# Linear attention followed by a squared-ReLU FFN: tokens tiled as 9p+j, K=64 matmuls in row groups, the max of k folded into v, the max of q subtracted in PSUM, the FFN interleaved with the next batch

## The chip, the cores and the metric

The kernel runs on one core of a Trainium2 chip (trn2). The metric is the device time of one execution in microseconds; lower is better. Executions of one kernel agree closely: the runs of the kernel before span 476.36 to 479.01 us in the rounds used here, about half a percent.

TensorE (PE in the profile) multiplies, DVE is VectorE, ACT is ScalarE, POOL is GpSimd. In these traces a matmul that waits holds up those issued after it: in the changed kernel PE stands idle for 1.32 us before the kv matmul at 83.11 us, which waits for scaled v, while FFN matmuls that need nothing from it come only afterwards, the first at 85.19 us. The order itself is chosen by the scheduler of the programming layer, which moves independent instructions into gaps that it expects.

## The reference, cut to what matters

```python
# q, k, v: (8 batches, 8 heads, 576 tokens, 64); w_phi: (64, 128)
def phi(x):
    proj = einsum('bhsd,df->bhsf', x, w_phi)
    proj = proj - max(abs(proj), axis=-1)          # over the 128 features
    return concatenate([exp(proj), exp(-proj)])
q_p, k_p = phi(q), phi(k)
kv  = einsum('bhsf,bhsd->bhfd', k_p, v);  z = sum(k_p, axis=2)
num = einsum('bhsf,bhfd->bhsd', q_p, kv); den = einsum('bhsf,bhf->bhs', q_p, z) + 1e-6
x   = (num / den) as (4608 tokens, 512)
out = relu(x @ w_in)**2 @ w_out                    # 512 -> 2048 -> 512
```

Subtracting m before both exponentials scales both halves of a token's features by exp(-m): exp(p-m) is exp(p) times exp(-m), but exp(-(p-m)) is exp(-p) times exp(+m). So the max of q is not a common factor of the two halves in the literal formula. The kernel before does not subtract it from q at all, and passes the comparison with the reference. The inputs (normal, times 0.1) make the maxima small. That is a property of this reference's data and tolerance, and it should be kept in mind.

## The kernel before

One batch has 576 tokens, cut in five chunks: four of 128 rows and one of 64. Per batch (cut):

```python
# transposes of q and k, two heads at a time; the fifth one has only 64 rows
for j, dstT in ((0, qT), (1, kT)):
    for pr in range(NPAIR):
        for isc, (s0, ssz) in enumerate(SCH):
            nc.tensor.transpose(out=tp[:, s0:s0+ssz], in_=xin[:ssz, isc, j, 2*pr:2*pr+2, :]..., ...)
        nc.scalar.activation(out=dstT[:, pr, :], in_=tp, func=ACT.Copy)
for isc, (s0, ssz) in enumerate(SCH):
    # 8 matmuls with K=64 -> pj; max; subtract; two Exp
    nc.vector.tensor_reduce(out=m[:ssz], in_=pj[:ssz], op=ALU.max, apply_absolute_value=True)
    nc.vector.tensor_tensor(out=ksh[:ssz], in0=pj[:ssz], in1=m..., op=ALU.subtract)
    nc.scalar.activation(out=kphp[:ssz, isc], in_=ksh[:ssz], func=ACT.Exp, scale=1.0)
    nc.scalar.activation(out=kphn[:ssz, isc], in_=ksh[:ssz], func=ACT.Exp, scale=-1.0)
    # 8 matmuls with K=64 -> pjq; two Exp of it; no max for q
    ...
    drain_op()            # one of the four FFN-out tiles (16 matmuls) of the chunk before
for hi in range(2):
    for pg in range(2):
        kv = ps.tile([P, 2, 2, D + 1], F32, tag="kv", bufs=2, ...)
        for pl in range(2):
            for pn, kph in ((0, kphp), (1, kphn)):
                for isc, (s0, ssz) in enumerate(SCH):      # K = 128,128,128,128,64
                    nc.tensor.matmul(out=kv[:, pl, pn, :],
                        lhsT=kph[:ssz, isc, hi, pr, :], rhs=va[:ssz, isc, h, :],
                        start=(isc == 0), stop=(isc == NSC - 1))
        nc.scalar.activation(out=kv_sb[...], in_=kv[...], func=ACT.Copy)
for isc, (s0, ssz) in enumerate(SCH):
    # 16 matmuls -> nd; reciprocal; multiply; 4 transposes -> xT
    ...
    if isc == ISC_RDY[b]:
        moe_hp(b)         # 64 FFN-in matmuls of 512 columns
```

Of the kernel before, what the change touches and what calls it, by code (L numbers as in the profile page):

```python
# [12 lines left out]
ACT = mybir.ActivationFunctionType  # L13


@with_exitstack
def kernel(
# [13 lines left out]
    Dh, Fd = w_phi.shape  # L31
    DM, DF = moe_w_in.shape
    NTOK = B * S
    P = 128
    NPAIR = H // 2
    KC1 = DM // P
    KC2 = DF // P
    SCH = [(i * P, min(P, S - i * P)) for i in range((S + P - 1) // P)]
    NSC = len(SCH)
    TCHUNK = 512  # L40
    NMC = NTOK // TCHUNK

    consts = ctx.enter_context(tc.tile_pool(name="consts", bufs=1))
    big = ctx.enter_context(tc.tile_pool(name="big", bufs=1))
# [4 lines left out]
    wphi2 = consts.tile([P, Fd], BF16)  # L49
    nc.gpsimd.dma_start(out=wphi2[0:Dh, :], in_=w_phi)  # L50
    nc.gpsimd.dma_start(out=wphi2[Dh : 2 * Dh, :], in_=w_phi)

    win = consts.tile([P, KC1, DF], BF16)
    wout = consts.tile([P, KC2, DM], BF16)

    def load_moe_weights():
        nc.gpsimd.dma_start(out=win, in_=moe_w_in.rearrange("(kc p) m -> p kc m", p=P))
        nc.gpsimd.dma_start(out=wout, in_=moe_w_out.rearrange("(kc p) n -> p kc n", p=P))

    xT = big.tile([P, KC1, NTOK], BF16)  # L60

    dmab = ctx.enter_context(tc.tile_pool(name="dmab", bufs=2))
    perb = ctx.enter_context(tc.tile_pool(name="perb", bufs=1))
    work = ctx.enter_context(tc.tile_pool(name="work", bufs=2))
    moeb = ctx.enter_context(tc.tile_pool(name="moeb", bufs=2))
    ps = ctx.enter_context(tc.tile_pool(name="ps", bufs=1, space=bass.MemoryType.PSUM))

    def load_inputs(b):
        xin = dmab.tile([P, NSC, 2, H, D], BF16, tag="xin")
        va = dmab.tile([P, NSC, H, D + 1], BF16, tag="va")  # L70
        nc.gpsimd.memset(va[:, :, :, D : D + 1], 1.0)  # L71
        for j, src in enumerate((q, k)):
            for isc, (s0, ssz) in enumerate(SCH):
                nc.gpsimd.dma_start(  # L74
                    out=xin[:ssz, isc, j],
                    in_=src[b, :, s0 : s0 + ssz, :].rearrange("h s d -> s h d"),
                )
        for isc, (s0, ssz) in enumerate(SCH):
            nc.gpsimd.dma_start(  # L79
                out=va[:ssz, isc, :, :D],  # L80
                in_=v[b, :, s0 : s0 + ssz, :].rearrange("h s d -> s h d"),
            )
        return xin, va

    pend = []

    def moe_hp(mc_i):
        t0 = mc_i * TCHUNK
        h2 = moeb.tile([P, KC2, TCHUNK], BF16, tag="h2", bufs=1)
        for mc in range(KC2):  # L90
            hp = ps.tile([P, TCHUNK], F32, tag="kv", bufs=2)
            for kc in range(KC1):
                nc.tensor.matmul(  # L93
                    out=hp,
                    lhsT=win[:, kc, mc * P : (mc + 1) * P],
                    rhs=xT[:, kc, t0 : t0 + TCHUNK],
                    start=(kc == 0), stop=(kc == KC1 - 1),
                )
            hr = moeb.tile([P, TCHUNK], BF16, tag="hr")
            nc.scalar.activation(out=hr, in_=hp, func=ACT.Relu)  # L100
            nc.vector.tensor_tensor(out=h2[:, mc], in0=hr, in1=hr, op=ALU.mult)
        for tt in range(TCHUNK // P):
            pend.append((mc_i, tt, h2))

    def moe_op(mc_i, tt, h2):
        t0 = mc_i * TCHUNK + tt * P
        op = ps.tile([P, DM], F32, tag="kv", bufs=2)
        for mc in range(KC2):
            nc.tensor.matmul(  # L109
                out=op, lhsT=h2[:, mc, tt * P : tt * P + P], rhs=wout[:, mc, :],  # L110
                start=(mc == 0), stop=(mc == KC2 - 1),
            )
        ot = moeb.tile([P, DM], F32, tag="ot", bufs=3)
        nc.vector.tensor_copy(out=ot, in_=op)  # L114
        nc.sync.dma_start(out=out[t0 : t0 + P, :], in_=ot)

    def drain_op():
        if pend:
            moe_op(*pend.pop(0))

    ISC_RDY = [(((bb + 1) * TCHUNK - 1) - bb * S) // P for bb in range(B)]

    nxt = load_inputs(0)
    load_moe_weights()

    for b in range(B):
        xin, va = nxt
        if b + 1 < B:
            nxt = load_inputs(b + 1)

        qT = perb.tile([P, NPAIR, S], BF16, tag="qT")
        kT = perb.tile([P, NPAIR, S], BF16, tag="kT")
        for j, dstT in ((0, qT), (1, kT)):
            for pr in range(NPAIR):
                tp = ps.tile([P, S], BF16, tag="t2", bufs=2,
                             padded_shape=[None, 1024])
                for isc, (s0, ssz) in enumerate(SCH):
                    nc.tensor.transpose(  # L138
                        out=tp[:, s0 : s0 + ssz],
                        in_=xin[:ssz, isc, j, 2 * pr : 2 * pr + 2, :].rearrange(  # L140
                            "s h d -> s (h d)"),
                        identity=ident[:ssz, :ssz],
                    )
                nc.scalar.activation(out=dstT[:, pr, :], in_=tp, func=ACT.Copy)  # L144

        kphp = perb.tile([P, NSC, 2, NPAIR, Fd], BF16, tag="kphp")
        kphn = perb.tile([P, NSC, 2, NPAIR, Fd], BF16, tag="kphn")
        qphp = perb.tile([Fd, 2, NPAIR, S], BF16, tag="qphp")
        qphn = perb.tile([Fd, 2, NPAIR, S], BF16, tag="qphn")
        for isc, (s0, ssz) in enumerate(SCH):  # L150
            pj = ps.tile([P, 2, NPAIR, Fd], F32, tag="pj", bufs=2)
            for hi in range(2):
                for pr in range(NPAIR):
                    nc.tensor.matmul(  # L154
                        out=pj[:ssz, hi, pr, :],
                        lhsT=kT[hi * Dh : (hi + 1) * Dh, pr, s0 : s0 + ssz],
                        rhs=wphi2[hi * Dh : (hi + 1) * Dh, :],
                        start=True, stop=True,
                    )
            m = work.tile([P, 2, NPAIR], F32, tag="m")  # L160
            nc.vector.tensor_reduce(out=m[:ssz], in_=pj[:ssz], axis=AX.X,  # L161
                                    op=ALU.max, apply_absolute_value=True)
            ksh = work.tile([P, 2, NPAIR, Fd], BF16, tag="ksh")
            nc.vector.tensor_tensor(out=ksh[:ssz], in0=pj[:ssz],  # L164
                                    in1=m[:ssz].to_broadcast([ssz, 2, NPAIR, Fd]),
                                    op=ALU.subtract)
            nc.scalar.activation(out=kphp[:ssz, isc], in_=ksh[:ssz],  # L167
                                 func=ACT.Exp, scale=1.0)
            nc.scalar.activation(out=kphn[:ssz, isc], in_=ksh[:ssz],  # L169
                                 func=ACT.Exp, scale=-1.0)  # L170
            pjq = ps.tile([Fd, 2, NPAIR, P], F32, tag="pj", bufs=2)
            for hi in range(2):
                for pr in range(NPAIR):
                    nc.tensor.matmul(  # L174
                        out=pjq[:, hi, pr, :ssz],
                        lhsT=wphi2[hi * Dh : (hi + 1) * Dh, :],
                        rhs=qT[hi * Dh : (hi + 1) * Dh, pr, s0 : s0 + ssz],
                        start=True, stop=True,
                    )
            nc.scalar.activation(out=qphp[:, :, :, s0 : s0 + ssz],  # L180
                                 in_=pjq[:, :, :, :ssz], func=ACT.Exp, scale=1.0)
            nc.scalar.activation(out=qphn[:, :, :, s0 : s0 + ssz],  # L182
                                 in_=pjq[:, :, :, :ssz], func=ACT.Exp, scale=-1.0)
            drain_op()

        kv_sb = perb.tile([P, 2, NPAIR, 2, D + 1], BF16, tag="kv_sb")
        for hi in range(2):
            for pg in range(2):
                kv = ps.tile([P, 2, 2, D + 1], F32, tag="kv", bufs=2,
                             padded_shape=[None, None, None, P])  # L190
                for pl in range(2):
                    pr = 2 * pg + pl
                    h = 2 * pr + hi
                    for pn, kph in ((0, kphp), (1, kphn)):
                        for isc, (s0, ssz) in enumerate(SCH):
                            nc.tensor.matmul(  # L196
# [9 lines left out]
        for isc, (s0, ssz) in enumerate(SCH):  # L206
# [31 lines left out]
            if isc == ISC_RDY[b]:  # L238
                moe_hp(b)
# [36 lines left out]
```

## Time and profile before

| | before |
|---|---|
| median of 3 runs (before the prediction) | 477.82 us (476.75 to 478.83) |
| span of the profiled run | 476.3 us |
| period of one batch | about 50.6 us |
| FFN matmuls, 128 per batch, 216 to 218 ns start to start | 28.2 us of each period |
| first FFN matmul | 58.7 us |

The page of the profile, parts 1 and 2: busy microseconds with their share of the span, then rows of 40 slices in which a digit is the busy share in tenths, and PEclk is the clock that TensorE was granted, in tenths.

```profile
PE 425.1 (89%) x3552; PEld 237.4 (50%) x3552; DVE 214.4 (45%) x340; ACT 301.8 (63%) x441; POOL 106.0 (22%) x138
...
PE   2533999999998999899989999899989997999996
...
PEclk9999999959997799869995999689976999699999
```

The same page's chain of work that ended last, by engine and then by line:

```profile
PE 73%; ACT 8%; DVE 8%; DMA 5%; POOL 4%; issue 1%; DVEq 0%; POOLq 0%; ACTq 0%
PE hp L93 23%; PE op L109 23%; PE kv L196 12%; DMA xin<-in_q_dram 5%; PE tp L138 4%; PE nd L211 3%; PE nd L216 3%; ACT kphp L167 3%; DVE ksh L164 2%; DVE m L161 2%; PE xtp L231 2%; POOL xin L74 2%; ACT qT L144 2%; ACT hr L100 1%; PE pj L154 1%
```

TensorE bounds the kernel. hp and op (the FFN) are 46% of the chain, and the first attention line is kv with 12%. Now the stretches of one period, by windows of time: length, then busy time and count on each engine, granted clock, share of DMA and GB/s. The first row is a period. The others follow one batch: transposes with the first half of kv, the second half of kv, and most of nd.

```profile
core 0: us, PE busy (x) PEld busy (x) DVE busy (x) ACT busy (x) POOL busy (x), PEclk, DMA share, GB/s
177.50:228.10 50.60, 48.88 (x431) 27.89 (x428) 25.62 (x41) 36.46 (x54) 12.83 (x16) 0.87 0.64 57
245.10:254.30 9.20, 7.48 (x85) 5.25 (x85) 3.03 (x3) 7.84 (x14) 0.00 (x0) 0.71 0.09 31
254.30:258.30 4.00, 4.00 (x42) 2.74 (x41) 0.00 (x0) 0.82 (x2) 0.00 (x0) 0.50 0.00 0
258.30:263.60 5.30, 5.24 (x82) 4.66 (x82) 2.59 (x7) 2.77 (x5) 4.87 (x7) 0.59 1.00 66
```

PE is "busy" all through the second half of kv, yet at half the clock and with 42 matmuls in 4.00 us. The timeline of PE shows a second reason beside the clock (start, length, engine, line, operation, operands, rows*columns of the weights, moving operand, count). This is a stretch at full clock, with a single K=64 matmul between groups of four with K=128:

```profile
44.51 0.23 PE L196 MATMUL kv<-va,kphp 64*128 64x65 bf16 x1
44.67 0.40 PE L196 MATMUL kv<-va,kphn 128*128 128x65 bf16 x4
45.01 0.23 PE L196 MATMUL kv<-va,kphp 64*128 64x65 bf16 x1
45.17 0.40 PE L196 MATMUL kv<-va,kphn 128*128 128x65 bf16 x4
```

A group of five takes 0.50 us (44.51 to 45.01), and the K=64 one alone holds 0.16 us until the next starts.

### The profile page before, as it was taken

What the parts mean: (1) busy time and instruction counts of PE and PEld (TensorE: products, weight loads), DVE (VectorE), ACT (ScalarE), POOL (GpSimd) and SP (SyncE); (2) the same over time, 40 slices, a digit from 0 to 9 for tenths busy, and PEclk for the clock granted to TensorE, in tenths of its full rate; (3) what the DMA queues carried; (4) which work ended last, traced back from release to release, by engine and by line L of the source; (5) the groups of instructions that cost most, each with busy time, mean ns of one, the idle gap of its engine ahead of it and who ended that gap; (6) DMA issues with size and microseconds to landing.
All of it is one profiled execution on the core that took longest, in us unless ns stands there. A gap on an engine that the chain in (4) does not pass through costs nothing.

```text
span 476.3 us, 8350 instructions
## 1 busy us (share of the span) xinstructions
PE 425.1 (89%) x3552; PEld 237.4 (50%) x3552; DVE 214.4 (45%) x340; ACT 301.8 (63%) x441; POOL 106.0 (22%) x138
## 2 busy tenths in 40 slices
PE   2533999999998999899989999899989997999996
PEld 1312744475445744574447554565456443644442
DVE  0360346716732457534661567156633575252331
ACT  2692578947946478946894678657883787371440
POOL 9804747028000730055002800030000000000000
PEclk9999999959997799869995999689976999699999
DMA  9999999619010991169011901070110011001101
GB/s 83 164 202 163 101 94 94 95 10 137 6 59 30 76 76 45 44 45 107 23 67 13 138 4 66 22 51 1 49 41 1 2 45 44 1 1 45 44 23 67
DMA packets 120485, 28.36 MB, mean 60 GB/s; under 512 B 113280, under 2 KB 115328, under 8 KB 120448
## 3 DMA queue, kind: packets, MB, share of 16 engines
q0 software_dynamic: 115264, 18.39, 53.0%
q1 hardware_dynamic: 5184, 9.44, 5.3%
q8 instruction: 28, 0.46, 0.4%
q14 instruction: 9, 0.07, 0.1%
HBM read 36.77 MB, written 9.44 MB: 97 GB/s over the span
## 4 chain that ended last, share of the span: by engine, by line
PE 73%; ACT 8%; DVE 8%; DMA 5%; POOL 4%; issue 1%; DVEq 0%; POOLq 0%; ACTq 0%
PE hp L93 23%; PE op L109 23%; PE kv L196 12%; DMA xin<-in_q_dram 5%; PE tp L138 4%; PE nd L211 3%; PE nd L216 3%; ACT kphp L167 3%; DVE ksh L164 2%; DVE m L161 2%; PE xtp L231 2%; POOL xin L74 2%; ACT qT L144 2%; ACT hr L100 1%; PE pj L154 1%
## 5 line engine op out<-in xcount | busy, mean ns | idle before, releaser
L93 PE MATMUL hp<-xT,win 128*128 128x512 bf16 x576 | 127.4, 379 | 0.7 <-ACT hr L100 0.2
L100 ACT ACTIVATE hr<-hp 128x512 bf16<-128x512 f32 x144 | 85.8, 599 | 55.4 <-PE hp L93 55.2
L93 PEld LDWEIGHTS <-win 128*128 128x128 bf16 x576 | 55.7, 98 | 66.9 <-issue 2.3
L138 PE MATMUL tp<-ident,xin 128*128 128x128 bf16 (+1 forms) x320 | 44.3, 255 | 30.5 <-DMA xin<-in_q_dram 18.9
L161 DVE TENSOR_REDUCE m<-pj 128x8 f32<-128x1024 f32 (+1 forms) x40 | 48.6, 1215 | 24.7 <-PE pj L154 24.7
L222 DVE RECIPROCAL rden<-nd 128x8 f32<-128x8 f32 (+1 forms) x40 | 8.1, 203 | 105.1 <-PE nd L216 104.7
L114 DVE COPY ot<-op 128x512 f32<-128x512 f32 x36 | 24.9, 692 | 59.4 <-PE op L109 59.4
L164 DVE TENSOR_TENSOR ksh<-pj,m 128x1024 bf16<-128x1024 f32 (+1 forms) x40 | 48.9, 1222 | 2.9
L167 ACT ACTIVATE kphp<-ksh 128x1024 bf16<-128x1024 bf16 (+1 forms) x40 | 42.3, 1058 | 11.9 <-DVE ksh L164 11.9
L138 PEld LDWEIGHTS <-xin 128*128 128x128 bf16 (+1 forms) x320 | 26.6, 110 | 43.6 <-DMA xin<-in_q_dram 20.6
L180 ACT ACTIVATE qphp<-pjq 128x1024 bf16<-128x1024 f32 (+1 forms) x40 | 37.2, 931 | 16.2 <-PE pjq L174 16.2
L71 POOL MEMSET va<- 128x40 bf16 x8 | 2.4, 300 | 178.0 <-PE kv L196 178.0
L169 ACT ACTIVATE kphn<-ksh 128x1024 bf16<-128x1024 bf16 (+1 forms) x40 | 41.9, 1048 | 0.0
L196 PE MATMUL kv<-va,kphp 128*128 128x65 bf16 (+1 forms) x320 | 36.1, 232 | 6.3 <-ACT kphp L167 6.2
L74 POOL DMA_DIRECT2D xin<-in_k_dram x40 | 34.2, 926 | 18.8 <-DMA wout<-in_moe_w_out_dram 10.4
L182 ACT ACTIVATE qphn<-pjq 128x1024 bf16<-128x1024 f32 (+1 forms) x40 | 37.6, 939 | 0.0
L74 POOL DMA_DIRECT2D xin<-in_q_dram x40 | 33.9, 908 | 9.1 <-PE tp L138 9.1
L196 PE MATMUL kv<-va,kphn 128*128 128x65 bf16 (+1 forms) x320 | 35.4, 240 | 0.2 <-ACT kphn L169 0.2
L202 ACT ACTIVATE kv_sb<-kv 128x260 bf16<-128x260 f32 x32 | 12.4, 388 | 35.5 <-PE kv L196 34.8
L79 POOL DMA_DIRECT2D va<-in_v_dram x40 | 33.7, 886 | 1.5 <-POOL va L71 1.5
L211 PE MATMUL nd<-kv_sb,qphp 128*128 128x65 bf16 (+1 forms) x320 | 33.3, 221 | 0.0
L216 PE MATMUL nd<-kv_sb,qphn 128*128 128x65 bf16 (+1 forms) x320 | 33.2, 222 | 0.0
(52 smaller groups left out, 528.4 us busy)
## 6 DMA issues: line engine op xcount, KB each, us to landing
out_dram<-ot SPq DMA_DIRECT2D x36, 256.0 KB, 2.0
xin<-in_q_dram POOLq DMA_DIRECT2D x32, 128.0 KB, 4.6
xin<-in_k_dram POOLq DMA_DIRECT2D x32, 128.0 KB, 4.6
va<-in_v_dram POOLq DMA_DIRECT2D x32, 128.0 KB, 5.0
win<-in_moe_w_in_dram POOLq DMA_DIRECT2D x1, 2048.0 KB, 15.0
wout<-in_moe_w_out_dram POOLq DMA_DIRECT2D x1, 2048.0 KB, 25.5
xin<-in_q_dram POOLq DMA_DIRECT2D x8, 64.0 KB, 4.2
xin<-in_k_dram POOLq DMA_DIRECT2D x8, 64.0 KB, 4.2
```

The source lines that it names most:

```text
L74: nc.gpsimd.dma_start(out=xin[:ssz, isc, j], in_=src[b, :, s0 : s0 + ssz, :].rearrange("h s d -> s h d"),)
L93: nc.tensor.matmul(out=hp, lhsT=win[:, kc, mc * P : (mc + 1) * P], rhs=xT[:, kc, t0 : t0 + TCHUNK], start=(kc == 0), stop=(kc == KC1 - 1),)
L100: nc.scalar.activation(out=hr, in_=hp, func=ACT.Relu)
L109: nc.tensor.matmul(out=op, lhsT=h2[:, mc, tt * P : tt * P + P], rhs=wout[:, mc, :], start=(mc == 0), stop=(mc == KC2 - 1),)
L138: nc.tensor.transpose(out=tp[:, s0 : s0 + ssz], in_=xin[:ssz, isc, j, 2 * pr : 2 * pr + 2, :].rearrange("s h d -> s (h d)"), identity=iden ...
L161: nc.vector.tensor_reduce(out=m[:ssz], in_=pj[:ssz], axis=AX.X, op=ALU.max, apply_absolute_value=True)
L164: nc.vector.tensor_tensor(out=ksh[:ssz], in0=pj[:ssz], in1=m[:ssz].to_broadcast([ssz, 2, NPAIR, Fd]), op=ALU.subtract)
L167: nc.scalar.activation(out=kphp[:ssz, isc], in_=ksh[:ssz], func=ACT.Exp, scale=1.0)
L169: nc.scalar.activation(out=kphn[:ssz, isc], in_=ksh[:ssz], func=ACT.Exp, scale=-1.0)
L196: nc.tensor.matmul(out=kv[:, pl, pn, :], lhsT=kph[:ssz, isc, hi, pr, :], rhs=va[:ssz, isc, h, :], start=(isc == 0), stop=(isc == NSC - 1),)
L211: nc.tensor.matmul(out=nd[:ssz, hi, pr, :], lhsT=qphp[:, hi, pr, s0 : s0 + ssz], rhs=kv_sb[:, hi, pr, 0, :], start=True, stop=False,)
L216: nc.tensor.matmul(out=nd[:ssz, hi, pr, :], lhsT=qphn[:, hi, pr, s0 : s0 + ssz], rhs=kv_sb[:, hi, pr, 1, :], start=False, stop=True,)
```

## The change

The intent: tile the 576 tokens as 9p+j (64 partitions, nine tokens each), so that a batch is nine blocks of 64 tokens without a remainder and DMA runs are 2304 bytes in place of 256; put two K=64 matmuls side by side in the two row groups; take reduction and subtraction of k's max out of the way of the exponentials by scaling v with exp(-m) and exp(+m); subtract q's max inside PSUM by a small matmul (the kernel before leaves it out); and issue the FFN of chunk c in small units between the steps of the attention of batch c+1. The core of the diff (cut):

```diff
-    SCH = [(i * P, min(P, S - i * P)) for i in range((S + P - 1) // P)]
+    NJ = S // 64
+    def rows(src, b):
+        return src[b].rearrange("(pr hi) (p j) d -> hi p pr (j d)", hi=2, j=NJ)
...
-            nc.vector.tensor_tensor(out=ksh[:ssz], in0=pj[:ssz], in1=m..., op=ALU.subtract)
-            nc.scalar.activation(out=kphp[:ssz, isc], in_=ksh[:ssz], func=ACT.Exp, scale=1.0)
+            absmax(mk, pj, nj, at)                    # DVE, no longer ahead of the Exp
+            nc.scalar.activation(out=kp[:, :, :w], in_=pj[:, :, :w], func=ACT.Exp, scale=1.0)
+            nc.scalar.activation(out=kn[:, :, :w], in_=pj[:, :, :w], func=ACT.Exp, scale=-1.0)
+            pj = project(qT[gi], nj)                  # only for the max of q
+            absmax(mq, pj, nj, at)
...
+        # va[s] = [v * exp(-/+ m), exp(-/+ m)]: six multiplications per batch on DVE
+                nc.vector.tensor_tensor(out=o[:, :, :, :D], in0=v0,
+                    in1=o[:, :, :, D].to_broadcast([P, 4, 4, D]), op=ALU.mult)
...
+                nc.tensor.matmul(out=pf[:, e, :w], lhsT=wphi2[r, :], rhs=qT[gi][r, :w],
+                    start=True, stop=False, skip_group_check=True)
+                    nc.tensor.matmul(out=pf[:, e, i * P : (i + 1) * P],      # minus max of q
+                        lhsT=nsel[r, at + i, :], rhs=mT[r, :], start=False, ...)
...
-                        for isc, (s0, ssz) in enumerate(SCH):
-                            nc.tensor.matmul(out=kv[:, pl, pn, :], lhsT=kph[:ssz, isc, hi, pr, :], ...)
+                        for hi in range(2):           # neighbours in different row groups
+                            r = slice(hi * 64, hi * 64 + 64)
+                            nc.tensor.matmul(out=kvv[:, hi, pr, : D + 1],
+                                lhsT=ph[s][r, e, i * Fd : (i + 1) * Fd], rhs=va[s][r, e, at + i, :], ...)
...
+        merge(a, 44, steps(ffn_units(c)), 16 if c in (0, NCH) else 32)
```

PSUM after the change: two "wide" accumulators of two banks each (projections, features, kv and numerators share them), one bank for transposes, two for FFN-in (hp) and one for FFN-out (op).

## The prediction

> **What bounds the kernel now.** TensorE. The chain of waits that ended last is 73% PE, and PE is busy 89% of 476.3 us. The timeline shows a strict period of about 50.6 us per batch (177.5 to 228.1): 64 FFN-in matmuls take 13.9 us and 64 FFN-out ones 4 x 3.57 us (218 ns start to start), so the FFN is about 28.2 us of it and 252 us of the whole; attention is the other 22.4 us. Most of that (245.1 to 263.6) has PE to itself, at a granted clock (windows) of 0.71, then 0.50 (kv), then 0.59 (nd), against 1.00 in the FFN stages. Start to start, nd takes 55 ns at clock 0.5 and 33 ns at full clock. A kv group of four K=128 matmuls and one K=64 takes 0.50 us, 0.22 us more than 5 x 55 ns: after the K=64 one, the next starts 0.16 us later. The Trainium skill ("TensorEngine Tiling (Array Packing)", Key Properties) says that changing the tiling mode drains TensorE; the trace agrees. The first FFN matmul starts at 58.7 us, after PE waited 10 us for the second batch's q.
>
> **What the change does.**
> - Start: larger DMA runs, no PE waiting for batch 1. Attention of batch 0 runs alone, limited by DVE then ACT: 8 us load + 17 (copies, 10 reductions of 1.22) + 4 + 4 + 14 (five groups of two Exp of 1.02, one copy of 0.6): first FFN at about 48 us, 10 earlier.
> - PE per batch, estimated at full clock from before: 40 transposes 2.5, 72 K=64 projections at 28 ns (eight took 0.22 us) 2.0, features 1.1 and subtraction 1.0, 144 kv at about 30 ns 4.3, 80 nd at 33 ns 2.6, 20 transposes 1.2, about 28 mode switches of 0.1 us (between FFN and K=64 units): about 17.5 us in place of 22.4.
> - Clock: with the FFN spread through attention, it should stay near 1.0.
> - DVE rises most: 80 reductions in place of 40 (49+49 to about 89 us, ksh gone), kT/qT copies moved from ACT (27 to 44), v scaling about 46 (1.2 us each if the broadcast keeps it at one element a cycle), h2 61, the rest 66: about 300 us, from 214. ACT falls from 302 to about 272.
>
> **Critical path.** In the projection half of a round, DVE needs about 24 to 26 us (copies, reductions, v scaling, FFN squares) against PE's 22 and scaled v must precede kv, so PE stalls. In the features half ACT (17) nearly matches PE (19). I put stalls at 3 to 6 us per round.
>
> Sum: 48 start + 252 FFN + 7 x 17.5 attention + 7 x 3.5 stalls + 4 end = 451 us.
>
> **Prediction: 451 us, 8 in 10 between 430 and 470.** Faster by over 2%: 0.83; within 2%: 0.13; slower: 0.04.
>
> **What would show the steps right or wrong.** First FFN matmul near 48 us. Round period 46 to 52 us. Granted clock above 0.95 after the start. kv matmuls about 30 ns apart, without gaps. DVE busy about 300 us, ACT about 272. PE waits mostly on DVE reductions and scaled v.
>
> **What would make it wrong.** Pairing worth more than 30 ns per matmul, and v scaling and PSUM copies at two elements a cycle, would take it to 430. Only two wide accumulators and one transposition buffer could stall the FFN behind DVE or ACT more than I allow; mode switches costing 0.2 us rather than 0.1 would add 20 us.

## The result, and the profile after

| | before | after |
|---|---|---|
| median, 4 runs each | 477.52 us | 458.44 us (458.01 to 458.86) |
| ratio, 95% interval | | 0.9595 (0.9577 to 0.9614) |
| first FFN matmul | 58.7 us | 54.9 us |
| period of one batch | 50.6 us | 46.0 us (start of kv to start of kv, six rounds, 44.3 to 48.0) |

Ratios in this text are the mean time of one kernel's fast runs over that of the other's of the same rounds, so they are not quite the ratio of the medians quoted.

The page after, parts 1 and 2:

```profile
PE 394.7 (86%) x4320; PEld 211.2 (46%) x4376; DVE 267.1 (58%) x465; ACT 252.0 (55%) x377; POOL 34.0 (7%) x58
...
PE   0646799799888998899899989998999899999975
...
PEclk9996599999999999999999999999999999999999
```

The clock row has what the change wanted: after the first batch TensorE is at full clock throughout. The chain that ended last:

```profile
PE 49%; DVE 29%; ACT 14%; issue 4%; DMA 2%; POOL 1%; ACTq 0%; another core or an unknown queue 0%; DVEq 0%; POOLq 0%
PE op L331 18%; PE hp L312 16%; DVE mk L153 5%; PE wide L280 4%; DVE mq L153 4%; DVE vp L202 4%; DVE vn L202 4%; ACT hr L317 3%; DVE xo L289 3%; ACT qp L242 3%; PE tp L129 3%; ACT qn L242 3%; PE xtp L297 2%; PE wide L144 2%; PE wide L258 2%
```

DVE has gained 21 points of the chain and PE has lost 24, through reductions (mk, mq) and the scaling of v (vp, vn). Three rounds by windows, from kv to kv:

```profile
core 0: us, PE busy (x) PEld busy (x) DVE busy (x) ACT busy (x) POOL busy (x), PEclk, DMA share, GB/s
172.40:216.80 44.40, 40.33 (x508) 22.20 (x515) 29.77 (x53) 28.17 (x42) 3.70 (x6) 1.00 0.36 65
216.80:263.00 46.20, 42.87 (x520) 22.98 (x527) 32.66 (x57) 29.82 (x45) 3.69 (x6) 1.00 0.35 63
263.00:308.80 45.80, 42.48 (x521) 23.02 (x527) 30.36 (x54) 29.97 (x45) 1.23 (x2) 1.00 0.19 37
```

And 72 kv matmuls, which the timeline now shows as one block:

```profile
80.51 1.28 PE L258 MATMUL wide<-vp,kp 64*128 64x65 bf16 x72
```

A sum over the trace says where the time went. For each matmul I take the time from its start to the start of the next one on PE, waits included, and add it up by what the matmul was. These sums, the time before the first matmul and the time after the last one's start make up the span.

| us from start to next start | before | after | difference |
|---|---|---|---|
| FFN | 252.9 | 271.7 | +18.8 |
| kv | 84.7 | 32.5 | -52.2 |
| transposes of q and k | 51.2 | 25.4 | -25.8 |
| projections, features, subtraction of q's max | 33.5 | 66.5 | +33.0 |
| numerators | 31.9 | 32.9 | +1.0 |
| transposes of x, and of the maxima | 11.6 | 15.0 | +3.4 |
| before the first matmul | 6.2 | 8.1 | +1.9 |

So two large gains, of which 16 us in the transposes are a DMA wait (18.9 us in the before trace, 2.6 after), stand against two large losses. A wait is put down to the matmul ahead of it, so the FFN's +18.8 is not slower FFN matmuls (216 ns in both) but what now waits behind them. Some matmul records are missing after (56 of the 1152 FFN ones); their time falls to their neighbours, mostly FFN too.

The theory at this point was: the gain is kv, and it could come from the pairing in row groups, from no longer changing between K=128 and K=64, or from the full clock that interleaving brings. The loss is the max of q, which the kernel before does not compute. The experiments take these apart.

### The profile page after: what moved, and what is told of

Its sections match the earlier page's. It is cut to its first block, busy times and chain, and to the rows that moved or that the text cites. A ratio compares the mean times of both kernels' runs of the same rounds, so it can differ in the third digit from the quotient of the medians.

```text
span 457.1 us, 9984 instructions
## 1 busy us (share of the span) xinstructions
PE 394.7 (86%) x4320; PEld 211.2 (46%) x4376; DVE 267.1 (58%) x465; ACT 252.0 (55%) x377; POOL 34.0 (7%) x58
## 4 chain that ended last, share of the span: by engine, by line
PE 49%; DVE 29%; ACT 14%; issue 4%; DMA 2%; POOL 1%; ACTq 0%; another core or an unknown queue 0%; DVEq 0%; POOLq 0%
PE op L331 18%; PE hp L312 16%; DVE mk L153 5%; PE wide L280 4%; DVE mq L153 4%; DVE vp L202 4%; DVE vn L202 4%; ACT hr L317 3%; DVE xo L289 3%; ACT qp L242 3%; PE tp L129 3%; ACT qn L242 3%; PE xtp L297 2%; PE wide L144 2%; PE wide L258 2%
## 5 line engine op out<-in xcount | busy, mean ns | idle before, releaser
L165 ACT ACTIVATE kp<-wide 128x1024 bf16<-128x1024 f32 (+1 forms) x40 | 37.5, 939 | 36.3 <-DVE mk L153 36.1
L242 ACT ACTIVATE qp<-wide 128x1024 bf16<-128x1024 f32 (+1 forms) x40 | 37.5, 937 | 34.2 <-PE wide L228 34.2
L153 DVE TENSOR_REDUCE mk<-wide 128x8 f32<-128x1024 f32 (+1 forms) x40 | 44.5, 1113 | 4.6 <-PE wide L144 4.6
L153 DVE TENSOR_REDUCE mq<-wide 128x8 f32<-128x1024 f32 (+1 forms) x40 | 44.4, 1110 | 0.5 <-PE wide L144 0.4
L242 ACT ACTIVATE qn<-wide 128x1024 bf16<-128x1024 f32 (+1 forms) x40 | 37.6, 941 | 0.0
L166 ACT ACTIVATE kn<-wide 128x1024 bf16<-128x1024 f32 (+1 forms) x40 | 37.5, 938 | 0.0
L280 PE MATMUL wide<-kv_sb,qp 128*128 128x65 bf16 (+1 forms) x320 | 31.8, 200 | 2.9 <-ACT qp L242 2.9
L280 PE MATMUL wide<-kv_sb,qn 128*128 128x65 bf16 (+1 forms) x320 | 26.8, 200 | 4.4 <-ACT qn L242 4.2
L280 PEld LDWEIGHTS <-qp 128*128 128x128 bf16 (+1 forms) x320 | 23.9, 103 | 12.7 <-ACT qp L242 8.4
L289 DVE TENSOR_TENSOR xo<-wide,rden 128x512 bf16<-128x512 f32 (+1 forms) x40 | 27.5, 689 | 1.2
```

Of the source, the lines that this page charges most:

```text
L153: nc.vector.tensor_reduce(out=m[:, :, at : at + w], in_=pj[:, :, : w * Fd].rearrange("x e (i f) -> x e i f", f=Fd), axis=AX.X, op=ALU.max, ...
L165: nc.scalar.activation(out=kp[:, :, :w], in_=pj[:, :, :w], func=ACT.Exp, scale=1.0)
L166: nc.scalar.activation(out=kn[:, :, :w], in_=pj[:, :, :w], func=ACT.Exp, scale=-1.0)
L242: nc.scalar.activation(out=o, in_=i_, func=ACT.Exp, scale=sg)
L280: nc.tensor.matmul(out=ndv[:m, h, : D + 1], lhsT=qph[s][:, h, :m], rhs=kv_sb[:, s, h % 2, h // 2, :], start=(s == 0), stop=(s == 1),)
L289: nc.vector.tensor_tensor(out=xo[:m].rearrange("t (h d) -> t h d", h=8), in0=ndv[:m, :, :D], in1=rden[:m].to_broadcast([m, 8, D]), op=ALU. ...
```

## The experiments

Twelve runs were made, of eleven kernels (a_best1 is a_noqmax again). "a_" names start from the changed kernel and "b_" names from the kernel before; times are medians of four runs, but a_seq and a_best1 were run once.

### a_seq: no interleaving

```diff
-        merge(a, 44, steps(ffn_units(c)), ...)
+        with tc.issue_after(mms[-1].ins):      # attention behind the last FFN matmul
+            for _ in a: pass
+        for _ in ffn_units(c): pass            # each FFN matmul kept at its place in PE's order
```

> The changed kernel with the interleaving undone: on TensorE each batch's attention is issued as one block, each FFN chunk as another. Theory (the gain is the interleaving: FFN matmuls fill attention's waits and keep the granted clock up): a round becomes 28 us of FFN plus an attention of 35 to 46 us, as the first batch took alone, so 560 to 640 us, slower than the kernel before. Rival (the cheaper attention itself makes the gain, the order matters little): 455 to 480 us.

Measured: 652.27 us (one look, result correct), mean granted clock 0.774. This is slower than expected and far from the rival. The new attention, by itself, is a chain of short steps from engine to engine; it is worth having only with other matmuls to put in the gaps. The kernel before also fills its attention with FFN-out tiles, so this does not say that interleaving is what separates the two.

### a_kvhalf: kv without pairing

```diff
-                for (j0, nj, at), ph in zip(groups, kph):
-                    for u in range(nj):
-                        for hi in range(2):
+                for hi in range(2):
+                    for (j0, nj, at), ph in zip(groups, kph):
+                        for u in range(nj):
```

> The changed kernel with the kv matmuls of the two 64-row halves issued one half after the other (9 and 9) in place of alternating, so that neighbours share a row group. If pairing in row groups gives the fast kv (20 ns per matmul), the spacing rises to about 30 ns and the time by 8 to 12 us, to about 468. If K=64 kv is fast only because nothing changes the tiling mode inside it and the clock is full, the time stays within 2 us of the changed kernel's.

Measured: 460.72 us, ratio 0.9636, against 0.9595 for the changed kernel: 2 us slower (459.92 to 461.10 us against 458.01 to 458.86), far from the 8 to 12 us of the first theory. The block of 72 that took 1.28 us takes 1.66 us in this kernel's timeline:

```profile
80.09 1.66 PE L258 MATMUL wide<-vp,kp 64*128 64x65 bf16 x72
```

In the blocks of 72 that nothing interrupts, all of them after the first batch, the starts are 15.3 to 15.4 ns apart on average with pairing and 20.4 to 20.6 ns without. With pairing they come two by two: 3 to 4 ns from the first of a pair to the second, 25 to 35 ns to the next pair. In the first batch the same matmuls are slower, about 27 and 33 ns, although the clock reads 1.00 there too; why was not tested. Pairing in row groups works, but over 1152 kv matmuls it is worth about 6 us of PE time (an estimate, 5 ns each) and 2 us of the kernel. It is not why kv fell by 52 us.

### b_kv128: the kernel before, with kv padded to K=128

```diff
+        nc.gpsimd.memset(va[S % P :, NSC - 1], 0.0)
...
+        nc.gpsimd.memset(kphp[S % P :, NSC - 1], 0.0)
+        nc.gpsimd.memset(kphn[S % P :, NSC - 1], 0.0)
...
-                                lhsT=kph[:ssz, isc, hi, pr, :], rhs=va[:ssz, isc, h, :],
+                                lhsT=kph[:, isc, hi, pr, :], rhs=va[:, isc, h, :],
```

> The kernel before, with the last chunk's kv matmul padded from 64 to 128 rows (zeros in v and in the features), so that every kv matmul has K=128. If the change of tiling mode costs 0.22 us per group of five, as read from the trace, each group falls from 0.50 to about 0.28 us and the time by 16 x 8 x 0.22 = 28 us less what was hidden: 450 to 462 us. If the half clock alone made kv slow, the time stays above 472 us.

Measured: 452.55 us, ratio 0.9468, correct. Filling 64 rows with zeros in the kernel before gains 25 us, more than the whole change does. In the sum over its trace kv falls from 84.7 to 60.2 us, which is all of the gain: inside kv, steps of 100 to 200 ns go from 222 (37.9 us) to 9 (1.4 us). So of the 52 us by which kv is cheaper in the changed kernel, about 25 are the alternation of K=128 and K=64. The other 28 go with a fuller clock (a step from K=128 to K=128 takes 34 ns at full clock in this kernel and 55 at half), fewer waits and the pairing, and were not taken apart further. Two groups of five in its timeline, at half clock, 0.27 us from one to the next in place of 0.50:

```profile
289.46 0.46 PE L199 MATMUL kv<-va,kphp 128*128 128x65 bf16 x5
289.73 0.47 PE L199 MATMUL kv<-va,kphn 128*128 128x65 bf16 x5
```

The padded kernel does more arithmetic and needs three more fills on POOL per batch.

### b_kvorder and b_kvzero: the kernel before, same kv matmuls in another order

Padding removes the change of mode, but also the K=64 matmul. So the next one keeps every matmul and only sorts them:

```diff
-                        for isc, (s0, ssz) in enumerate(SCH):           # 128,128,128,128,64
-                            nc.tensor.matmul(out=kv[:, pl, pn, :], ..., start=(isc == 0), stop=(isc == NSC - 1))
+                        for isc, (s0, ssz) in enumerate(SCH[:-1]):      # all K=128 of this accumulator
+                            nc.tensor.matmul(out=kv[:, pl, pn, :], ..., start=(isc == 0), stop=False, ...)
+                for pl in range(2):                                     # then its four K=64
+                    for pn, kph in ((0, kphp), (1, kphn)):
+                        nc.tensor.matmul(out=kv[:, pl, pn, :], ..., start=False, stop=True, ...)
```

> The kernel before with the same kv matmuls in another order: in each of the four accumulators of a batch, first the sixteen K=128 ones, then the four K=64 ones. Nothing is padded or left out; the changes between K=128 and K=64 inside kv fall from 32 to 8 per batch. If the change of tiling mode is what costs (0.22 us per group of five, two changes each), 12 of 16 pairs of changes go: 12 x 8 x 0.22 = 21 us, 455 to 462 us. If the K=64 matmul is slow in itself, nothing changes: 475 to 479 us.

Measured: 443.72 us, ratio 0.9297, but the result was wrong (relative error 4.76). The Trainium skill ("PSUM — Partial Sum Buffer", The four PSUM rules, rule 2) says that the first matmul of an accumulation clears the "has written" bits of the whole 2 KiB bank, and a later one overwrites where the bit is clear. Four accumulations share a bank here, so three of them lost their sums when the next one started, which the wrong result agrees with. The mended kernel starts the bank once, with zeros:

```diff
+                nc.tensor.matmul(out=kv, lhsT=ident, rhs=zeros, start=True, stop=False, ...)
...
-                                start=(isc == 0), stop=False, skip_group_check=True,
+                                start=False, stop=False, skip_group_check=True,
```

> The reordered kv of b_kvorder again, made right: its result was wrong because the start of one accumulation in a PSUM bank makes the others in that bank begin again. Here one matmul with zeros starts the whole bank and all others add. 32 more matmuls of 260 columns, 0.11 to 0.22 us each, so at most 4 to 7 us more than b_kvorder's 443.7: 444 to 451 us, and a right result. If the wrong result had made b_kvorder fast, the time returns to 470 us or more.

Measured: 443.40 us, ratio 0.9297 (0.9256 to 0.9338), correct. Its timeline, one accumulator: the start with zeros, sixteen K=128 matmuls, four K=64.

```profile
277.57 0.29 PE L193 MATMUL kv<-zeros,ident 128*128 128x260 bf16 x1
277.69 0.29 PE L202 MATMUL kv<-va,kphp 128*128 128x65 bf16 x4
277.82 0.29 PE L202 MATMUL kv<-va,kphn 128*128 128x65 bf16 x4
277.94 0.33 PE L202 MATMUL kv<-va,kphp 128*128 128x65 bf16 x4
278.08 0.41 PE L202 MATMUL kv<-va,kphn 128*128 128x65 bf16 x4
278.42 0.23 PE L213 MATMUL kv<-va,kphp 64*128 64x65 bf16 x1
278.47 0.24 PE L213 MATMUL kv<-va,kphn 64*128 64x65 bf16 x1
```

The K=64 matmuls follow each other at 0.05 us, at a clock that has fallen by then; the K=64 matmul was never slow in itself. What was slow is the step between the two kinds. In the before trace the median from one kv start to the next is 54 ns from K=128 to K=128 (half clock, mostly), 178 ns from K=128 to K=64 and 165 ns from K=64 to K=128. The last two are the same at full clock (14 and 15 steps) as at half clock (96 and 90), so the half clock is not what made them long. This is what the Trainium skill ("TensorEngine Tiling (Array Packing)", Key Properties) calls the drain at a change of tiling mode. One period of this kernel, to set against the 50.60 us at 0.87 of before:

```profile
284.80:331.10 46.30, 43.84 (x404) 25.21 (x409) 24.62 (x38) 35.05 (x52) 0.41 (x1) 0.93 0.19 32
```

46.3 us, as the changed kernel's rounds, with DVE at 24.6 us per round in place of 30 to 33. A second effect is inside the 34 us: numerators, which this edit does not touch, come at a median of 33 ns in place of 54, as the clock is granted more often. The order also lets kv start before the last chunk's exponentials are done, and spares POOL the fills of b_kv128; how the 9 us between the two kernels divide over these was not separated.

### a_noqmax: without the max of q

```diff
-            pj = project(qT[gi], nj)
-            absmax(mq, pj, nj, at)
...
-        nc.tensor.transpose(out=mtp, in_=mp..., identity=ident)       # and all that makes mp, mT, nsel
...
-                        lhsT=nsel[r, at + i, :], rhs=mT[r, :],
```

> The changed kernel without the max of q: its projections, reductions, transposition and the subtraction in PSUM are left out (the kernel before never had them; they cancel in the quotient but for the 1e-6). If TensorE's issue slots bound the rounds, this frees about 19 us of q projections, 19 us of subtraction and 2 us of transposition, besides 44 us of DVE: 410 to 425 us. If the waits between the engines bound the rounds instead, less than half of it comes back: above 438 us.

The edit also hands the interleaving 38 attention steps per batch in place of 44, as six are gone. Measured: 433.56 us, ratio 0.9069, correct; on another chip (a_best1) 432.79 us.

One remark in that expectation is wrong, that the maxima cancel in the quotient: as the section on the reference says, q's max scales the two halves of the features by exp(-m) and exp(+m), so it is no common factor. What holds is only that this kernel, like the one before, leaves it out and still agrees with the reference.

> One more look at a_noqmax for its trace, on the same chip as the combination after it: 431 to 436 us.

The max of q costs 25 us, less than expected and more than the rival allowed. Where the estimate failed: it counted 19 us for the subtraction, from the sum over the trace. But features and subtraction together only fell from 28.2 to 16.5 us, since the time of the change back to K=128 matmuls stayed and now follows the features. The projections fell from 38.3 to 22.0 us, the transposition's 1.8 us went. That is 30 us, and a new wait takes back a part of it. About 6 of the 25 us are gained before the first FFN matmul, which starts at 48.8 us in place of 54.9. PE's waits after the start, in all, number and longest, in this kernel:

```profile
PE hp L273 <- ACT hr L278: 7.4, 7, 1.6
PE wide L219 <- DVE vn L177: 5.8, 4, 1.5
```

The first of these was 0.2 us in the changed kernel: with less to do between FFN matmuls, FFN-in now waits for its own ReLU on ACT.

### a_ksub and a_ksub2: the max of k subtracted again

```diff
+            nc.vector.tensor_tensor(out=ksh[...], in0=pj[...], in1=mk[...].to_broadcast(...), op=ALU.subtract)
-            nc.scalar.activation(out=kp[:, :, :w], in_=pj[:, :, :w], func=ACT.Exp, scale=1.0)
+            nc.scalar.activation(out=kp[:, :, :w], in_=ksh[:, :, :w], func=ACT.Exp, scale=1.0)
...
-                nc.vector.tensor_tensor(out=o[:, :, :, :D], in0=v0, in1=..., op=ALU.mult)   # six per batch
+            nc.vector.tensor_copy(out=o[:, :, :, :D], in_=v0)                                # three per batch
```

> The changed kernel with the max of k subtracted before the Exp, as in the kernel before, in place of folded into v (v is only copied). DVE gets 40 subtractions of up to 1.22 us and loses 48 scalings of up to 1.22 us, 0.4 us each for the copies. Theory: the fold moves work and saves none, so 452 to 464 us, with the waits of kv for v gone and new ones for the subtraction. Rival: the fold is a large part of the gain, since it takes reduction and subtraction out of the way of the Exp: above 468 us.

Measured: 490.12 us, ratio 1.0254, correct. That contradicted my theory, but the trace had a flaw: the scheduler had moved the copies of v up, and DVE stood 26.8 us in front of them, waiting for v's loads. So once more with the copies kept in place:

> a_ksub again with the three copies of v kept at their place in DVE's order. In a_ksub DVE waited 26.8 us for v's loads at copies that the scheduler had put too early. If that wait made the 490 us, this takes 455 to 466 us and the fold of the max into v is worth at most 2 percent. If the fold itself is the gain, it stays above 480 us.

Measured: 485.87 us, ratio 1.0172, correct. The flaw was worth 4 us. a_ksub2 is within 2% of the kernel before, which the changed kernel beats by 4%. The fold of the max into v is worth 27 us (485.87 less 458.44), more than the change as a whole, and my theory that it only moves work is refuted. All instructions of DVE together take as long as in the changed kernel (busy 269.9 against 267.1 us), so the place matters, not the amount. One round of each, split at the first transpose of the next batch: first the half with copies, projections and reductions, then the half with kv, features and numerators. The changed kernel:

```profile
241.40:263.00 21.60, 20.57 (x177) 10.34 (x180) 19.89 (x31) 13.42 (x21) 2.46 (x4) 1.00 0.46 81
263.00:287.00 24.00, 21.41 (x342) 12.75 (x346) 11.53 (x24) 16.06 (x24) 1.23 (x2) 1.00 0.26 48
```

a_ksub2:

```profile
255.60:280.40 24.80, 20.69 (x176) 10.05 (x180) 22.47 (x35) 13.02 (x18) 2.44 (x4) 0.99 0.38 65
280.40:307.80 27.40, 25.94 (x348) 15.17 (x354) 9.61 (x23) 16.96 (x26) 1.48 (x3) 0.89 0.27 51
```

In both kernels DVE is busy 91 to 92% of the first half and half idle or more in the second. The first half is as long as DVE needs. The subtraction must stand there, between reduction and Exp; half of the scaling (that for the negative exponentials) may be done while kv of the positive ones runs, in the half where DVE has room. Kv to kv is 50 to 52 us in a_ksub2 from the third batch on, against 44 to 48. Both first halves hold 66 FFN matmuls (counted by PE's weight loads), so there the comparison is clean. The second half is longer too, but half of its 3.4 us is FFN work: a_ksub2 has 63 FFN matmuls in it and the changed kernel 55, at 216 ns each. The rest comes at a clock of 0.89 in place of 1.00; whether that clock follows from PE's longer waits in the first half is likely but was not tested.

### a_nd0 and a_tail: the two ends

a_nd0 gives the first batch's numerators the two hp banks, which no FFN uses yet; a_tail lets the last chunk's FFN-out tiles alternate between op and hp.

```diff
+            if b == 0:
+                nds = [ps.tile([P, 512], F32, tag="hp", bufs=2, name="nd0")... for _ in range(2)]
...
+            last = c == NCH - 1 and tt % 2 == 1
+            op_ps[0] = ps.tile([P, DM], F32, tag="hp" if last else "op", bufs=2 if last else 1, name="op")
```

> The changed kernel with the first batch's numerator tiles in the two hp accumulators, which are idle then, so that the wide ones serve the features alone. If the first batch's group period of 4.5 us comes from features and numerators taking turns in two wide accumulators, it falls to 3 to 3.5 us (two Exp, one copy on ACT, 2.7 us at least) and the first FFN matmul starts 4 to 7 us earlier than 54.9 us: 452 to 455 us. If ACT or something else sets the period, the time stays within 1 us.

Measured: 450.30 us, ratio 0.9432, correct. ACT's timeline in the first batch shows the turn-taking. The changed kernel, one group of features and the wait ahead of it:

```profile
44.07 1.02 ACT L242 ACTIVATE qp<-wide 128x1024 bf16<-128x1024 f32 x1 [2.07 <-PE wide L228]
44.99 0.59 ACT L303 ACTIVATE xT<-xtp 128x512 bf16<-128x512 bf16 x1
45.46 1.03 ACT L242 ACTIVATE qn<-wide 128x1024 bf16<-128x1024 f32 x1
```

a_nd0, where ACT has no gap:

```profile
39.44 1.02 ACT L242 ACTIVATE qp<-wide 128x1024 bf16<-128x1024 f32 x1
40.36 0.59 ACT L313 ACTIVATE xT<-xtp 128x512 bf16<-128x512 bf16 x1
40.83 1.03 ACT L242 ACTIVATE qn<-wide 128x1024 bf16<-128x1024 f32 x1
41.82 0.60 ACT L313 ACTIVATE xT<-xtp 128x512 bf16<-128x512 bf16 x1
42.31 1.02 ACT L242 ACTIVATE qp<-wide 128x1024 bf16<-128x1024 f32 x1
```

qp to qp is 2.87 us here against 4.5. The first FFN matmul comes at 47.2 us in place of 54.9, and no slice of the page's clock row is below 9. That clock is not the cause: one of the changed kernel's four runs had a mean clock of 1.00 as well and took 458.44 us. The gain of 8 us (runs of 449.02 to 453.32) is a little above the expected 4 to 7.

> The changed kernel with the last four FFN-out tiles alternating between the single op accumulator and the idle hp ones. The trace has three waits of 0.8 us there for the copy of the only op accumulator; they go, so 1.6 to 2.6 us less than the changed kernel (456 to 457 us).

Measured: 454.78 us, ratio 0.9513, correct: 3.7 us less where I expected 1.6 to 2.6. The first FFN matmul of this profile is 0.5 us later than in the changed kernel's, so the gain is not from the start. The expectation had counted one wait too few: after 430 us PE waits four times for the copy in the changed kernel's trace, 0.88 us once and 0.78 three times, together 3.2 us, and not once in this one. That leaves half a microsecond.

### a_best2: what goes together

a_noqmax with a_nd0 and a_tail.

> The changed kernel without the max of q, with the first batch's numerators in the idle accumulators and the last FFN-out tiles in two of them. If the three gains are on the critical path independently, 458.4 - 25 - 8 - 3.6 = 422 us (418 to 427). If the start's gain needs the q max's waits, about 428 us.

Measured: 425.36 us, ratio 0.8901 (0.8873 to 0.8928), correct. The sum of the three gains holds within 4 us. This is the fastest kernel. It is not the same function as the changed kernel in its use of q's max (see the section on the reference), but the same as the kernel before's in that respect.

| kernel | us | ratio to before |
|---|---|---|
| before | 477.5 to 478.3 | 1 |
| a_ksub2 | 485.87 | 1.0172 |
| a_kvhalf | 460.72 | 0.9636 |
| changed kernel | 458.44 | 0.9595 |
| a_tail | 454.78 | 0.9513 |
| b_kv128 | 452.55 | 0.9468 |
| a_nd0 | 450.30 | 0.9432 |
| b_kvzero | 443.40 | 0.9297 |
| a_noqmax | 433.56 | 0.9069 |
| a_best2 | 425.36 | 0.8901 |

Not in the table: a_seq (652.27, one look), a_ksub (490.12, with the misplaced copies) and b_kvorder (443.72, wrong result).

## Why the prediction was right, point by point

- **Time.** 451 us predicted, 430 to 470 as the range, 458.44 measured, and faster by 4%. Right. Its sum was 48 for the start, 399 for everything from the first FFN matmul on, and 4 for the end. The trace has 54.9, 397.6 (to the end of the last matmul at 452.5) and 4.6. The miss of 7 us is the start.
- **Start, mis-sized.** The text has "14 (five groups of two Exp of 1.02, one copy of 0.6)". That is ACT's time for the groups, taken as if ACT had no waits; a group took 4.5 us, not 2.8, because features and numerators take turns in two accumulators and PE is in order. a_nd0 shows it: with two more banks qp to qp is 2.87 us and the first FFN matmul comes at 47.2 us.
- **Rounds.** "Round period 46 to 52 us" was right, 46.0. The sum behind it has 28.2 of FFN + 17.5 attention + 3.5 stalls = 49.2. The 46.0 comes about because the scheduler let the FFN fall behind: by PE's order six rounds have 716 FFN matmuls, 119 each and not 128, which is 25.8 us at 216 ns. That leaves 20.2 for attention and stalls together, where the prediction had 21.0.
- **Granted clock above 0.95 after the start.** Right: 1.00 in the rounds shown.
- **kv about 30 ns apart, no gaps.** Better than that, 15 ns in an unbroken block after the first batch; between the positive and the negative half PE waits up to 1.3 us for the scaled v.
- **DVE about 300 us, ACT about 272.** Added up by instruction, the trace has 289 and 277. The page counts overlapping instructions once and has 267 and 252. Copies of bf16 out of PSUM took 0.69 us for 1024 elements and 0.29 for 256, so 768 elements take 0.40 us; 512 elements of a reduction take 0.53 (1.22 less 0.69). The copies are twice as fast per element, which was the better of the two cases I allowed; the scaling of v is not.
- **"PE waits mostly on DVE reductions and scaled v."** Half right. After the first FFN matmul PE's waits are, by the profile:

```profile
PE op L331 <- DVE ot L337: 6.2, 10, 0.9
PE xtp L297 <- DVE xo L289: 5.6, 18, 0.6
PE wide L258 <- DVE vn L208: 5.3, 4, 1.3
PE wide L258 <- DVE vn L202: 2.8, 3, 0.9
```

  Scaled v is there with 8.1 us, the reductions hardly (0.2 us): the scheduler put FFN matmuls where they would have been waited for. They show up as DVE's share of the chain instead.
- **What the prediction did not price.** It read the 0.22 us per kv group and cited the drain for it, but never multiplied: 128 groups are 28 us, and that one term is more than the 19 us the whole change gained. b_kv128 gains 25 us by taking it away; b_kvzero gains 34, with the clock's share in it. Nor did it set the work for q's max apart from the rest; a_noqmax puts it at 25 us. The total could come out right all the same because the new attention was added up afresh: a large gain and a large loss that I had not named were both inside "17.5 in place of 22.4". That they nearly cancelled was not foreseen.

## What to carry to other kernels

Before rebuilding a kernel, look at the start-to-start times inside the blocks of small matmuls, and sort or pad so that K=64 and K=128 matmuls do not alternate: here that edit of a few lines in the old kernel gained 34 us, more than the rebuild's 19. When a normalisation can be moved through a product, as k's max into v, ask in which stage the engine that does it has room; the same DVE time in another place made 27 us of difference here, a lower granted clock included. And price what a rewrite adds for fidelity separately from what it does for speed, as the two can hide each other in the total.

## What the Trainium skill lacked or had wrong

- "TensorEngine Tiling (Array Packing)", Key Properties, says that a change of mode drains TensorE, but not what it costs: 165 to 178 ns from start to start here, where matmuls of 65 columns without a change came at 33 ns (full clock) to 54 ns (half).
- The same page gives up to 2x for two row tiles. With 64 rows, 128 weight columns and 65 moving columns, pairing took the mean spacing from 20.4-20.6 ns to 15.3-15.4 ns, about 1.3x.
- "TensorE: Matmul & The Clock Gate", Part 1, has about 25 ns as the least time from start to start however few the columns. K=64 matmuls of 65 columns came at 20.4 to 20.6 ns on average in a_kvhalf, where eight of nine neighbours share a row group.
- "VectorE: DVE Perf Modes", the perf-mode tier table, has tensor_tensor on bf16 in SBUF at two elements a cycle. The scaling of v, whose second operand is broadcast, took 0.42 us for 256 elements, as long as the FFN square took for 512. The page does not name broadcast operands, but its condition for that rate, step ±1 in every tensor, leaves them out, so this is not missing there.
- "PSUM — Partial Sum Buffer", rule 2, was right where it mattered: accumulations that were interleaved in one bank gave a wrong result (relative error 4.76), and one start for the bank mended it.
